# Batch 1's k and q permutes made available 0.7 later in the planner's list for ScalarE, in an attention kernel with a two-layer MLP

## The chip, the cores and the metric

The kernel runs on one core of one Trainium2 chip. The metric is the device time of one execution in microseconds. A lower time is better. The profile is one execution of the same program, taken by the hardware profiler; its span runs from the first to the last profiled instruction.

## The reference

Inputs are q, k and v with 8 batches, 8 heads, 576 rows and head width 64, a norm gain of width 64, a layer-norm gain of width 512 and two weight matrices of 512 x 2048 and 2048 x 512, all in float32. Cut to what matters:

```python
kv  = einsum('bhsd,bhse->bhde', k, v)          # 64 x 64 per batch and head
out = einsum('bhsd,bhde->bhse', q, kv)
out = out / sqrt(mean(out*out, -1) + 1e-6) * g_norm
x   = out.transpose(0, 2, 1, 3).reshape(8, 576, 512)
xn  = (x - mean(x)) / sqrt(var(x) + 1e-6) * g_ln
y   = x + maximum(xn @ w_ch1, 0) @ w_ch2       # 8 x 576 x 512
```

## The kernel before, in words

The 8 x 576 = 4608 rows are cut into 36 tiles of 128 rows. Each batch gives four full tiles, and the last 64 rows of two neighbouring batches share a fifth one (`TILES`, lines 75 to 79). Tiles 0 to 3 belong to batch 0, tiles 4 to 7 to batch 1, tile 8 holds the two fifths, and tile 9 is the first of batch 2. Four tiles make a block. Blocks 0 and 1 are "fine": their first MLP layer runs tile by tile (`m1_fine`, L629, 16 matmuls of 128 columns per group). Later blocks run it for four tiles at once (`m1_block`, L644). The second layer is `m2` (L663, four matmuls of 512 columns per group).

A batch needs these steps ahead of the MLP. Its k, v and q are loaded by DMAs that POOL issues and that convert to bf16. For batches 0 to 2 the loads put several rows of one head side by side, and a copy then permutes them to the order the matmuls need: `k_permute` (L404, into `kp`) and `q_permute` (L410, into `qp`), both through the helper `copy`, so that all of them show as L400 on ScalarE. `kv_mm` (L456, matmuls at L461) multiplies k with v, and `kv_out` (L469) puts the result into `kv_pack`. The q tiles are transposed, on TensorE with a copy out of PSUM (`q_turn_pe`, L420, and `q_turn_out`, L400 or L402) or by a transposing DMA that SP issues (`q_turn_dma`, L442). Then `t_out` (L484) multiplies the turned q with `kv_pack`, and squares (`t_sq`, L510), their sums (L519), a root (L523), the scaling (L546 or L550) and the centring (L572) give `xc`. This is turned to `xT` (L579 and L586 for tiles 0 to 11, a DMA at L590 later), which is the input of the first layer. `t_s2` (L596, tile `junk`) takes squares for the variance.

For batch 1, `plan_batch` makes two `k_permute` steps of four heads each, keyed `p - 18`, and four `q_permute` steps of one tile each, keyed `p - 17`, `p - 14`, `p - 11` and `p - 8`, where p is 32. Tiles 0 and 1 of q are turned on TensorE: VectorE copies the first out of PSUM and ScalarE the second. Tiles 2 and 3 are turned by one DMA, which needs the last two permutes. The buffer `qb` that these permutes read is loaded again for batch 2 once the last of them has read it (`qread`, line 774); batch 2's two q permutes (line 789) wait for that load with a lag of 4.0.

The order on each engine is not written out by hand. Every step is given to `add` with an engine, the time that it holds the engine (`occ`), the time until its result can be used (`dur`), a key and its dependencies, and `run_plan` (L108) plays the program through with these estimates. At each turn it takes, over all engines, the step that could start first. On one engine, among steps that could start at the same moment, the lowest key wins. A step that could start up to 0.35 later (`NEAR`) is preferred where its key is lower by more than 0.7 and the other step would get in its way; on PE this holds only for keys below -3. Between keys 16 and 32 the main matmul groups go strictly in their order. DMAs are modelled as one server that works them off in order of issue (`server`). Where a step depends on a DMA, its `lag` is added to the modelled landing:

```python
r = max(r, d.done + (s.lag if d.dma else 0.0))
```

The steps are then emitted in order of their planned start, so the plan fixes only the order on each engine and each DMA queue. On the chip each instruction runs when its engine has come to it and its data are there. PSUM has four banks for matmul groups (tag `mm`), two for `out` and two for `kvt`, and a step that takes a bank also waits for the step that frees it (`frees`).

Of the kernel before, what the change touches and what calls it, by code (L numbers as in the profile page):

```python
# [14 lines left out]
def kernel(  # L15
# [11 lines left out]
    nc = tc.nc  # L27
# [38 lines left out]
    def no_fifth(b):  # L66
        return fifth(b + 1)
# [30 lines left out]
    def add(eng, occ, dur, key, deps, fn, dma=None, alloc=None, main=False, lag=0.0):  # L98
        s = Step()
        s.eng, s.occ, s.dur, s.key, s.fn = eng, occ, dur, key, fn  # L100
        s.deps = [d for d in deps if d is not None]
        s.dma, s.alloc, s.main, s.frees, s.behind = dma, alloc, main, None, None
        s.start = s.done = None
        s.lag = lag
        steps.append(s)
        return s
# [80 lines left out]
    def act_cost(n):  # L187
        return n / 1400 + 0.115, n / 1400 + 0.23
# [51 lines left out]
    def kv_view(buf, b):  # L240
        if b < 2:
            return buf[b % 2][0:96, :].rearrange("p (h t d) -> p h t d", h=H, t=6)
        return buf[b % 2][:, 0:H * 4 * D].rearrange("p (h t d) -> p h t d", h=H, t=4)
# [43 lines left out]
    lag = [("a", 4), ("a", 5), ("b", 4), ("a", 6), ("b", 5), ("a", 7), ("b", 6), ("b", 7)]  # L287
# [59 lines left out]
    def pool_do(occ, fn, deps=()):  # L347
        return add("POOL", occ, occ + 0.1, 0, deps, fn)
# [49 lines left out]
    def copy(eng, o, i):  # L398
        if eng is nc.scalar:
            eng.copy(o, i)  # L400
        else:
            eng.tensor_copy(o, i)  # L402

    def k_permute(eng, b, h0, h1):  # L404
        src = kv_view(kb, b)
        t = src.shape[2]
        copy(eng, kp[b % 2][0:src.shape[0], 0:t, h0:h1, :],
             src[:, h0:h1, :, :].rearrange("p h t d -> p t h d"))

    def q_permute(eng, b, t0, t1):  # L410
        copy(eng, qp[b % 2][:, t0:t1, :, :],
             qb[:, :, t0:t1, :].rearrange("p h t d -> p t h d"))
# [15 lines left out]
    def add_q_turn_pe(b, t, deps, key, eng, h0=0, h1=H):  # L428
        w = (h1 - h0) / H
        s = add("PE", 0.24 * w, 0.24 * w + 0.26, key, [ident] + list(deps), lag=2.0 if t == 4 else 0.0, fn=  # L430
                lambda: q_turn_pe(b, t, h0, h1), alloc=("mm", "kvt")[b])
        occ, dur = act_cost(512 * w) if eng == "ACT" else dve_cost(512 * w, 1.92)
        e = add(eng, occ, dur, key, [s],
                lambda: q_turn_out(b, t, h0, h1, nc.scalar if eng == "ACT" else nc.vector))
        s.frees = e
        adone[b].setdefault(("qT", t), []).append(e)
        return s
# [10 lines left out]
    def add_q_turn_dma(b, t0, t1, deps, key):  # L448
        s = add_dma("SP", key, deps, lambda: q_turn_dma(b, t0, t1), 520.0 * (t1 - t0), 1.0,
                    occ=0.6 * (t1 - t0) + 0.1, lat=0.25, tail=0.42)  # L450
        for t in range(t0, t1):
            adone[b].setdefault(("qT", t), []).append(s)
        if t0 == 4:
            late_turns.append(s)
# [266 lines left out]
    def plan_batch(b):  # L721
        p = pos[FIRST[b]]
        ok = okey[FIRST[b]]
        kperm = []
        if b == 1:
            for h0, h1 in ((0, 4), (4, 8)):
                kperm.append(add("ACT", 1.2, 1.35, p - 18, load["k", 1],
                                 lambda h0=h0, h1=h1: k_permute(nc.scalar, 1, h0, h1)))
            for t in range(5):
                key = (p - 17 + 3 * t) if t < 4 else pos[8] - 40  # L730
                if t < 4:
                    qperm = add("ACT", *act_cost(512), key, load["q", 1],
                                lambda t=t: q_permute(nc.scalar, 1, t, t + 1))
                    qread = qperm
                else:
                    qperm = load["q", 1, 4][0]
                if t < 2:
                    add_q_turn_pe(1, t, [qperm, z1[1]], key + 1, ("DVE", "ACT")[t % 2])
                elif t > 2:
                    add_q_turn_dma(1, *((2, 4) if t == 3 else (4, 5)), [qperm, z1[1]],  # L740
                                   key + 1 if t == 3 else pos[8] - 29)
            vdeps = load["v", 1]
            adone[1]["qread"] = qread
            adone[1]["qfree"] = adone[1]["qT", 4][0]
        else:
            f = FIRST[b]
            def gate(n):

                if b >= 3:
                    m, i = divmod(n, 4)  # L750
                    pool_do(0.1, lambda: nc.gpsimd.tensor_copy(  # L751
                        mark, blk[m]["xT"][:, 0, i * 128:i * 128 + 1]), done[n]["xT"])
            def gate_turn():
                if b >= 3:
                    pool_do(0.1, lambda: nc.gpsimd.tensor_copy(
                        mark, att[b - 1]["qT"][:, 0, 0:1]), [adone[b - 1]["qfree"]])
            dk = [adone[b - 2]["kvmm"]]
            if b < 4:

                pool_do(0.5, lambda: nc.gpsimd.memset(kp[b % 2][no_fifth(b), 4, :, :], 0.0), dk)  # L760
            gate(f - 8 if b > 3 else 5)
            gate_turn()
            by_slot = b >= 3
            if by_slot:
                pool_load(("k", b), load_slots(kp[b % 2], k, b), rate1, dk)
            else:
                pool_load(("k", b), load_kv(kb, k, b), rate4, dk)
            pool_load(("k", b), load_fifth(kp[b % 2][:, 4, :, :], k, b), 180.0, dk)
            def some_q():
                gate(f - 7 if b > 3 else 6)  # L770
                if by_slot:
                    pool_load(("q", b), load_slots(qp[b % 2], q, b), rate1, [adone[b - 2]["qfree"]])
                else:
                    pool_load(("q", b), load_q(b, 0, 4), rate4, [adone[b - 1]["qread"]])
                pool_load(("q", b), load_fifth(qp[b % 2][:, 4, :, :], q, b), 180.0,
                          [adone[b - 2]["qfree"]])
            def some_v():
                gate(f - 6 if b > 3 else 7)
                pool_load(("v", b), load_kv(vb, v, b), rate4, dk)
                pool_load(("v", b), load_fifth(v5[b % 2], v, b), 100.0, dk)  # L780
            for load_some in (some_v, some_q) if b == 2 else (some_q, some_v):
                load_some()
            for h0, h1 in ((0, 4), (4, 8))[by_slot * 2:]:
                kperm.append(add("ACT", 0.85, 1.0, ok - 16, load["k", b][0:1] + dk,
                                 lambda h0=h0, h1=h1: k_permute(nc.scalar, b, h0, h1)))
            qperm = []
            for t0, t1 in ((0, 2), (2, 4))[by_slot * 2:]:
                qperm.append(add("ACT", 0.85, 1.0, ok - 14, load["q", b][0:1] + [
                    adone[b - 2]["qfree"]], lambda t0=t0, t1=t1: q_permute(nc.scalar, b, t0, t1)))
            for x in kperm + qperm:  # L790
                x.lag = 4.0 if b == 2 else 6.0
            kperm += load["k", b]
            turn = add_dma("SP", ok - 12, qperm + load["q", b] + (
                adone[b - 3].get("outs", []) if b >= 3 else []),
                           lambda: q_turn_dma(b), 2.6e3, 1.0, occ=2.98, lat=0.25, tail=0.42)
            for t in range(5):
                adone[b]["qT", t] = [turn]
            adone[b]["qfree"] = turn
            turn.lag = 5.0 if by_slot else 0.0
            adone[b]["qread"] = qperm[-1] if qperm else None  # L800
            vdeps = load["v", b]
        outs_before = adone[b - 3].get("outs", []) if b >= 3 else []
        s = add("PE", 1.12 if b > 1 else 1.34, 1.35 if b > 1 else 1.57, (p - 17.5 if b == 1 else ok - 4), vdeps + kperm,
                lambda: kv_mm(b, range(HP)), alloc="kvt")
        a = add("DVE", 0.34, 0.38, (p - 17 if b == 1 else ok - 2), [s, z1[4], z1[5]] + outs_before,
                lambda: kv_out(b, 0, HP, nc.vector, False))
        a2 = add("DVE", 0.34, 0.38, (p - 17 if b == 1 else ok - 2), [a], lambda: kv_out(b, 0, HP, nc.vector, True))
        s.frees = a2
        s.lag = 5.0 if b > 2 else 2.0 if b == 2 else 0.0
        adone[b]["kvmm"] = s  # L810
        adone[b]["kv"] = [a2]
# [243 lines left out]
```

## Time and profile before

| what | value |
| --- | --- |
| median of 4 runs | 293.45 us (292.79 to 294.83) |
| the profiled execution's own time | 293.36 us |
| its span | 291.6 us |
| PE busy | 284.2 us (97%) |
| PE weight loads busy | 161.7 us (55%) |
| DVE busy | 165.0 us (57%) |
| ACT busy | 142.5 us (49%) |
| POOL busy | 66.4 us (23%) |
| granted TensorE clock | 0.999 |

The page names engines as PE (TensorE), PEld (its weight loads), DVE (VectorE), ACT (ScalarE), POOL (GpSimd) and SP (SyncE, which here only issues DMAs). A line of a timeline gives the start, the duration, the engine, the source line, the operation, the tile it writes and the tile it reads; an idle time ahead of it stands in brackets with what ended it. The chain of work that ended last is followed back from the last instruction. PE's matmul ends are modelled, so the distance between the starts of two groups says more than the end of one.

### The profile page before, as it was taken

The page shows a single profiled execution, that of the slowest core. Times are in us where ns is not written, and L with a number is a line of the kernel's source. Part 1 is how long each engine was busy: PE and PEld are TensorE (multiplying, and loading weights), DVE is VectorE, ACT ScalarE, POOL GpSimd, SP SyncE. Part 2 cuts the span into 40 slices and gives each one's busy share as a digit, 9 for nine tenths or more (in the row PEclk, how much of TensorE's full clock was granted, in tenths as well). Part 3 has the DMA queues.
Part 4 walks back from the last instruction along what each step waited for, and adds up shares of the span by engine and source line. Part 5 has one row for each costly group of instructions (what it writes and reads, how often), then busy time and mean ns, then how long its engine had stood idle before and what let it go on. Part 6 is the DMA issues. An engine that isn't in the chain of part 4 may idle for free.

```text
span 291.6 us, 5221 instructions
## 1 busy us (share of the span) xinstructions
PE 284.2 (97%) x2074; PEld 161.7 (55%) x2074; DVE 165.0 (57%) x362; ACT 142.5 (49%) x288; POOL 66.4 (23%) x93
## 2 busy tenths in 40 slices
PE   8889999999999999999999999999999999999995
PEld 6779845977645445444544445444544444444444
DVE  2586039487973997557755775477557755320022
ACT  2379954788756512761276126612761177016400
POOL 8974231007309005403160405000000000000000
PEclk9999999999999999999999999999999999999999
DMA  7999999948999989996999299912101310120012
GB/s 97 182 199 205 204 199 180 243 78 98 182 222 92 170 117 193 133 176 152 133 132 190 64 202 112 181 55 92 54 18 56 90 54 18 58 93 13 2 72 73
DMA packets 108716, 35.60 MB, mean 122 GB/s; under 512 B 87187, under 2 KB 104467, under 8 KB 108692
## 3 DMA queue, kind: packets, MB, share of 16 engines
q0 software_dynamic: 72624, 18.35, 67.6%
q1 hardware_dynamic: 35828, 16.79, 25.6%
q8 instruction: 16, 0.26, 0.3%
q10 hardware_dynamic: 240, 0.13, 0.2%
q14 instruction: 8, 0.07, 0.1%
HBM read 36.70 MB, written 9.44 MB: 158 GB/s over the span
## 4 chain that ended last, share of the span: by engine, by line
PE 85%; DMA 7%; POOL 6%; issue 0%; ACT 0%; DVE 0%; POOLq 0%
PE mm_ps L663 41%; PE mm_ps L644 33%; DMA qb<-in_q_dram 7%; PE mm_ps L629 5%; PE out_ps L484 3%; PE kv_ps L461 2%; POOL qp L270 1%; POOL w L354 1%; POOL vb L249 1%; POOL kb L249 1%; PE xT_ps L579 1%; POOL w L356 1%; PE qT_ps L420 0%; ACT qp L400 0%; POOL identity masks.py:197 0%
## 5 line engine op out<-in xcount | busy, mean ns | idle before, releaser
L663 PE MATMUL mm_ps<-w,m 128*128 128x512 bf16 (+2 forms) x608 | 129.6, 368 | 0.0
L644 PE MATMUL mm_ps<-xT,w 128*128 128x512 bf16 x448 | 100.6, 379 | 0.0
L651 ACT ACTIVATE m<-mm_ps 128x512 bf16<-128x512 f32 x112 | 66.8, 598 | 50.8 <-PE mm_ps L644 49.9
L663 PEld LDWEIGHTS <-m 128*128 128x128 bf16 x608 | 57.2, 98 | 60.6
L644 PEld LDWEIGHTS <-w 128*128 128x128 bf16 x448 | 43.1, 98 | 48.9
L519 DVE TENSOR_REDUCE ss<-sq 128x8 f32<-128x512 f32 (+1 forms) x37 | 24.8, 670 | 48.1 <-ACT sq L510 48.0
L670 DVE SCALAR_TENSOR_TENSOR x<-mm_ps,rstd,x 128x512 f32<-128x512 f32 (+2 forms) x38 | 27.3, 719 | 40.6 <-PE mm_ps L663 40.6
L510 ACT ACTIVATE sq<-out_ps 128x512 f32<-128x512 f32 (+1 forms) x37 | 21.6, 584 | 45.5 <-PE out_ps L484 45.5
L629 PE MATMUL mm_ps<-xT,w 128*128 128x128 bf16 x512 | 30.6, 219 | 0.0
L629 PEld LDWEIGHTS <-w 128*128 128x128 bf16 x512 | 29.2, 98 | 0.8
L572 DVE SCALAR_TENSOR_TENSOR xc<-x,mv,gl 128x512 bf16<-128x512 f32 (+1 forms) x38 | 27.3, 723 | 1.2
L514 DVE TENSOR_TENSOR xg<-out_ps,gn 128x512 f32<-128x512 f32 x34 | 23.2, 683 | 0.2
L636 ACT ACTIVATE m<-mm_ps 128x512 bf16<-128x512 f32 x32 | 18.4, 598 | 3.0 <-PE mm_ps L629 2.9
L751 POOL COPY mark<-xT 128x1 bf16<-128x1 bf16 x15 | 6.9, 460 | 56.3 <-DMA xT<-xc 50.8
L523 ACT ACTIVATE rms<-ss,eps_attn 128x8 f32<-128x8 f32 (+1 forms) x37 | 11.1, 300 | 14.5 <-DVE ss L519 14.5
L550 DVE TENSOR_TENSOR x<-xg,inv 128x512 f32<-128x512 f32 x24 | 16.6, 692 | 0.8
L566 DVE BATCH_NORM_STATS2 stats<-x 128x6 f32<-128x512 f32 x24 | 16.6, 690 | 0.5
L484 PEld LDWEIGHTS <-qT 128*128 128x128 bf16 x160 | 11.4, 98 | 6.8 <-ACT qT L400 0.8
L484 PE MATMUL out_ps<-kv_pack,qT 128*128 128x128 bf16 x160 | 14.5, 219 | 0.4 <-ACT qT L400 0.3
L472 DVE CAST kv_pack<-kv_ps 64x256 bf16<-64x256 f32 x14 | 5.9, 422 | 11.9 <-PE kv_ps L461 11.8
L461 PEld LDWEIGHTS <-kp 128*128 128x128 bf16 (+1 forms) x168 | 10.1, 98 | 2.5 <-issue 0.4
L277 POOL DMA_DIRECT2D qp<-in_q_dram x5 | 11.2, 2235 | 0.8 <-issue 0.8
(69 smaller groups left out, 181.6 us busy)
## 6 DMA issues: line engine op xcount, KB each, us to landing
out_dram<-x SPq DMA_DIRECT2D x30, 256.0 KB, 2.6
w<-in_moe_w_ch_dram POOLq DMA_DIRECT2D x8, 512.0 KB, 12.4
vb<-in_v_dram POOLq DMA_DIRECT2D x6, 512.0 KB, 10.9
kp<-in_k_dram POOLq DMA_DIRECT2D x5, 512.0 KB, 8.6
qp<-in_q_dram POOLq DMA_DIRECT2D x5, 512.0 KB, 10.1
out_dram<-x SPq DMA_DIRECT2D x10, 128.0 KB, 2.3
qb<-in_q_dram POOLq DMA_DIRECT2D x2, 512.0 KB, 18.5
qp<-in_q_dram POOLq DMA_DIRECT2D x10, 64.0 KB, 9.2
```

The source lines that it names most:

```text
L484: nc.tensor.matmul(o3[:, hp, :], lhsT=att[b]["qT"][:, 4 * t + hp, :], rhs=kv_pack[b % 3][:, hp, :], start=(i == 0), stop=(i == len(bs) - 1))
L510: nc.scalar.activation(sq[:, h0:h1, :], st[n]["ps", h0][:, h0:h1, :], func=AF.Square)
L514: nc.vector.tensor_mul(xg[:, h0:h1, :], st[n]["ps", h0][:, h0:h1, :], gn.to_broadcast([128, h1 - h0, D]))
L519: nc.vector.tensor_reduce(ss[:, h0:h1, :], st[n]["sq"][:, h0:h1, :], axis=AX.X, op=ALU.add)
L550: nc.vector.tensor_mul(x, xg, inv)
L572: nc.vector.scalar_tensor_tensor(xc[:, f0:f1], in0=st[n]["x"][:, f0:f1], scalar=blk[m]["mv"][:, i, 0:1], in1=gl[:, f0:f1], op0=ALU.subtrac ...
L629: nc.tensor.matmul(ps[:, d, :], lhsT=w1[c][:, kk, d * 128:(d + 1) * 128], rhs=blk[m]["xT"][:, kk, i * 128:(i + 1) * 128], start=(kk == 0), ...
L636: nc.scalar.activation(st[n]["m1"][:, c, :, :], st[n]["m1ps", c], func=AF.Relu)
L644: nc.tensor.matmul(ps, lhsT=w1[c][:, kk, d * 128:(d + 1) * 128], rhs=blk[m]["xT"][:, kk, :], start=(kk == 0), stop=(kk == nKm - 1))
L651: nc.scalar.activation(blk[m]["m1", c][:, d, :], blk[m]["m1ps", g], func=AF.Relu)
L663: nc.tensor.matmul(st[n]["m2ps", f0], lhsT=m1_piece(n, c, d), rhs=w2[c][:, d, f0:f1], start=(c == 0 and d == 0), stop=(c == 3 and d == 3))
L670: nc.vector.scalar_tensor_tensor(x[:, f0:f1], in0=st[n]["m2ps", f0], scalar=blk[m]["rstd"][:, i, :], in1=x[:, f0:f1], op0=ALU.mult, op1=AL ...
```

## The change

The two k permutes and the four q permutes of batch 1 get `lag=0.7`, where they had none. The planner then takes their data to be there 0.7 after the modelled landing of the load. No instruction is added or removed, and no cost estimate or key is altered. Everything that differs on the chip is an order of instructions on the engines and queues, as far as the planner comes to another one.

```diff
         if b == 1:
             for h0, h1 in ((0, 4), (4, 8)):
                 kperm.append(add("ACT", 1.2, 1.35, p - 18, load["k", 1],
-                                 lambda h0=h0, h1=h1: k_permute(nc.scalar, 1, h0, h1)))
+                                 lambda h0=h0, h1=h1: k_permute(nc.scalar, 1, h0, h1), lag=0.7))
             for t in range(5):
                 key = (p - 17 + 3 * t) if t < 4 else pos[8] - 40
                 if t < 4:
                     qperm = add("ACT", *act_cost(512), key, load["q", 1],
-                                lambda t=t: q_permute(nc.scalar, 1, t, t + 1))
+                                lambda t=t: q_permute(nc.scalar, 1, t, t + 1), lag=0.7)
                     qread = qperm
```

## The prediction

> **What bounds the kernel now.** I read the page first: span, busy shares and the chain's shares.
>
> ```profile
> span 291.6 us, 5221 instructions
> ...
> PE 284.2 (97%) x2074; PEld 161.7 (55%) x2074; DVE 165.0 (57%) x362; ACT 142.5 (49%) x288; POOL 66.4 (23%) x93
> ...
> PE 85%; DMA 7%; POOL 6%; issue 0%; ACT 0%; DVE 0%; POOLq 0%
> ```
>
> PE is the bound. Next, the chain in order of time, around the place the change touches.
>
> ```profile
> 18.97 0.24 issue
> 19.21 19.70 DMA qb<-in_q_dram
> 38.91 0.02 issue
> 38.93 0.63 ACT qp L400
> 39.56 0.05 issue
> 39.61 0.40 PE qT_ps L420 x4
> 40.00 0.86 PE mm_ps L663 x4
> 40.87 0.22 PE out_ps L484 x4
> ```
>
> From 39.61 to 288.06 every piece of the chain is PE, one after the other. So a microsecond of new PE idleness after 39.61 costs a microsecond, and nothing there can be won by order. The only thing to win is the step before it: PE waits for the first q permute of batch 1, which waits for a load. Third, the timelines of PE and ACT.
>
> ```profile
> 33.28 1.03 PE L663 MATMUL mm_ps<-w,m 128*128 128x512 bf16 x4
> 34.14 1.50 PE L461 MATMUL kv_ps<-vb,kp 96*128 96x128 bf16 x24
> 35.49 3.62 PE L663 MATMUL mm_ps<-w,m 128*128 128x512 bf16 x16
> 39.61 0.40 PE L420 MATMUL qT_ps<-identity,qp 128*128 128x128 bf16 x4 [0.50 <-ACT qp L400]
> ```
>
> ```profile
> 29.50 1.09 ACT L636 ACTIVATE m<-mm_ps 128x512 bf16<-128x512 f32 x2
> 30.90 1.47 ACT L400 COPY kp<-kb 96x1536 bf16<-96x1536 bf16 x1 [0.31 <-DMA kb<-in_k_dram]
> 32.28 1.07 ACT L636 ACTIVATE m<-mm_ps 128x512 bf16<-128x512 f32 x2
> 33.24 1.46 ACT L400 COPY kp<-kb 96x1536 bf16<-96x1536 bf16 x1
> 38.93 2.17 ACT L400 COPY qp<-qb 128x512 bf16<-128x512 bf16 x4 [1.55 <-DMA qb<-in_q_dram]
> 41.35 0.59 ACT L400 COPY qT<-qT_ps 128x512 bf16<-128x512 bf16 x1 [0.24 <-PE qT_ps L420]
> 60.05 1.99 ACT L400 COPY qp<-qb 128x1024 bf16<-128x1024 bf16 x2
> ```
>
> PE's idle time: a group of four L663 matmuls takes 0.864 (the chain's 1.73 for eight), so sixteen from 35.49 are issued by 38.95; the next instruction starts at 39.61. That is 0.66 us, of which the bracket counts 0.50 after the modelled end. The ACT rows show both loads landing with ACT already idle: 0.31 for k, 1.55 for q.
>
> **The new order, worked by hand.** The change acts through the planner, so I carried its rules through by hand from the costs in the code. Its dates (called "planned") serve to find the order only; durations below are the profile's. In the old plan k lands at 30.19 and q at 38.27, while the trace has 30.9 and 38.91: the plan is 0.65 to 0.7 early, and the lag moves it there.
>
> *k permutes.* The first becomes possible at planned 30.95 instead of 30.25. The eviction of tile 3's first MLP group is possible at 31.06 with key 13 against 14, inside the 0.35 window, so it goes first. On ACT the order becomes eviction, permute, eviction, permute, two evictions. From the rows: PE gives tile 3's first group at 28.81 + 2 x 0.893 + 0.2 (latency to ACT, as at L636's waits) = 30.8; eviction pitch 0.48; permute pitch 1.38 (30.90 to 32.28). The permutes start at 31.28 and 33.14, and the second ends at 34.60 (34.70 before). The eviction fills ACT's 0.31 idle; the sum on ACT is 0.1 us shorter, and no PE wait depended on it.
>
> *kv product.* Its planned readiness moves from 34.26 to 34.63, past the end of the first `m2` group at 34.32, so the second `m2` group goes ahead of it. On the chip: `m2` 34.14, kv at 35.00 to 36.35, with its inputs there since 34.60. Its copies to `kv_pack` (two, 0.86 together) end near 37.6; `t_out` of tile 4 needs them after 41. Cost nothing, cover 3 us.
>
> *q permutes.* Planned 39.03 instead of 38.33. PE has a free turn at 39.12 with nothing but the next `m2` group to run; the first q turn goes behind it. PE before: m2, turn 0, m2, out 4, turn 1, m2, m2, out 5. After: m2, m2, turn 0, turn 1, m2, out 4, out 5, m2. On the chip the moved group runs 38.94 to 39.80, over the whole wait. Turn 0 has its data (39.56). Turn 1 comes at 40.02 and needs the second permute: starts are (2.17 - 0.61)/3 = 0.52 apart, so it ends at 38.93 + 0.52 + 0.61 = 40.06, and with 0.05 to PE it is a wait of 0.09. Out 4 at 41.20 needs VectorE's copy of turn 0 (39.80 + 0.43 + 0.42 = 40.65), out 5 at 41.42 ScalarE's copy of turn 1 (40.11 + 0.42 + 0.59 = 41.12). Both are there.
>
> So PE gains 0.66 - 0.09 = 0.57 us. Bounds: 0 if another wait follows at once, and 0.86 (the whole moved group) in an execution where q lands later than 38.91.
>
> *What moves with them: the last q permute, SP and POOL.* ScalarE's copy of turn 1 (key 19 against 24) goes ahead of the fourth permute, which then runs 41.01 to 41.62 instead of ending at 41.10. Two queues wait for it: SP's transposing DMA of q tiles 2 and 3, and POOL's load of batch 2's q into the same buffer.
>
> ```profile
> 41.13 1.33 SPq L442 DMA_TRANSPOSE qT<-qp  x1
> ```
>
> ```profile
> 42.03 0.89 POOL L256 DMA_DIRECT2D qb<-in_q_dram  x1 [1.59 <-ACT qT L400]
> ```
>
> The transpose is issued 0.5 later. Issue to landing of these was 5.0 to 8.8 us in this trace, so it is there by 50.5; `t_out` 6 runs after 53. No cost. The load was issued 0.93 after the permute ended and may now be issued between 41.65 and 42.55; it took 17.3 us to land (59.33), and its readers started at 60.05.
>
> In the planner the swap counts for more. Old planned starts: SP's transpose 40.42, the load 40.79 (held by its DMA lane). New: both at the same instant, and the tie goes to POOL, which is looked at first. The modelled server then puts the 2.66 us load ahead of the transpose. Planned landing of q tiles 2 and 3 goes from 52.56 to 55.22, and batch 2's q gets there 1.04 sooner. Two orders follow. `t_out` 6 and 7 go behind two more groups on PE (53.36 before; 55.46 after, in chip time less the 0.57). ScalarE's squares of tile 6 move from 55.39 to about 55.9, `xc` of tile 6 ends near 59.8, and its turn has its place at 60.70 - 0.57 = 60.13: covered by 0.3. And batch 2's two q permutes are placed on ScalarE before `junk` of tile 5 and the squares of tile 7, about 1 us earlier. On the chip they will then wait for the load: issued at 42.0, landed at 59.3, permutes until 61.25 (1.89 for two), `junk` 0.63, copy of `xT` 6 0.59, so 62.5. Tile 6's first group wants it at 63.51 - 0.57 = 62.94. Covered by 0.45.
>
> One more tight place: VectorE takes y of tiles 1 and 2 ahead of `xc` of tile 5; y of tile 3, which frees a bank, ends near 51.75 against 51.89 for the group that takes the bank. Between 0 and 0.2 us; I take 0.
>
> A rule of the Trainium skill bears on the swap. The rows are the landing times above: the short transposes land in 5.0 to 8.8 us while the loads beside them take 17.3 or more, so a transpose does not stand behind a whole load. DMA: Bandwidth & Descriptors, section Queues, rings and completion order, says that each DMA engine goes round-robin over queue rows, a packet at a time. By the rows the swap costs nothing, as taken; by the planner's single server it would put q tiles 2 and 3 up to 2.66 us later, still ahead of 53, so the sum stays.
>
> A second rule speaks against the change: TensorE: Matmul & The Clock Gate, section Architectural detail, calls ScalarE's queue strictly first-in, first-out. What stands behind batch 2's permutes then cannot pass while they wait for their load; the trace shows such a stop at 38.93 (1.55 idle). By the rule with no cover, the wait from 58.4 to 59.3 would come off the gain, 293.8; with the cover of 0.45 worked out above it stays 292.9.
>
> **The sum.** The profiled execution took 293.36 us, 1.76 outside its span of 291.6. 293.36 - 0.57 = 292.79; the median of the runs lies 0.09 above that execution: about 292.9 us. A difference under 0.5% (1.47 us) is about what a measurement here can't tell from no change, so this is "same".
>
> **The rivals.**
>
> *Nothing moves or the wait only changes place.* If PE's 0.66 us goes to another wait right behind (turn 1, the bank of y 3, `xT` 5), the time is 293.2 to 293.5. For it: covers of 0.1 to 0.45 are thin. Against: three rows would have to be late together. 12%.
>
> *Slower: batch 2's q permutes stop ScalarE.* Place: ScalarE from about 58.4 (60.05 less 1.04 and 0.57); behind them `xT` 6. The stall on PE is (landing - 59.80), one to one. It decides against the change at a landing of 59.80 + 0.57 = 60.37, and makes over 0.5% at 61.84. The other load into this buffer took 19.70 instead of 17.3: issued at 42.03 that is 61.73, a stall of 1.93, and 293.36 + 0.09 - 0.57 + 1.93 = 294.8; issued at 42.55 it is 295.3. For it: the planner believes in 54.66 plus a lag of 4.0 where the chip had 59.33. Against: 17.3 is this load's own row, and the page shows the DMA engines running dry just then, so that the landing is set by what is queued and not by a few tenths of issue time. The slice with the 4 begins at 58.3 us (40 slices of 7.29):
>
> ```profile
> DMA  7999999948999989996999299912101310120012
> ```
>
> With the many orders after 60 that also change and that I can't all follow (each wait there is paid in full), 15% for over 0.5%.
>
> *Faster by over 0.5%.* It needs 1.47 us, and PE has 0.66 of idleness left to remove, 0.86 with a late q. Only a run-to-run difference gets there: 5%.
>
> **Numbers.** The forecast's case, 68%, own range 292.4 to 293.2. Same 68 + 12 = 80%, slower 15%, faster 5%. The 8-in-10 range goes from 292.2 (gain 0.86 and the spread of runs, lowest 0.66 under their median) to 294.8 (the stall by the longer load).
>
> **What would show it.** Right: the PE timeline has two `m2` groups before the kv product, four after it, then both q turns together and no bracket at the first; the chain no longer passes through the q load; `t_out` 6 and 7 stand near 55.5. Wrong: a bracket at L629 near 63 that names `xT`, a bracket at L484 near 67 that names SP's transpose, or the first q turn still waiting for ScalarE. The prediction fails if the planner, by a tie that I resolved wrongly, orders blocks 1 and 2 so that PE meets a new wait of over 2 us.

## The result, and the profile after

The changed kernel takes 293.9 us (median, 292.96 to 297.02) against 293.17 us for the kernel before, measured beside it. The ratio is 1.0023, with a 95% interval of 1.0014 to 1.0032: a loss of 0.7 us, inside the 0.5% that was called "same", but a loss where a gain of 0.6 was forecast. The profiled execution took 293.65 us, 1.75 outside its span. The profiled executions of two kernels below, e12 and g1, ran at a granted clock of 0.758 and 0.564, so no profile of these two is used.

The page of the changed kernel, span, busy shares and the chain's shares:

```profile
span 291.9 us, 5221 instructions
...
PE 285.6 (98%) x2074; PEld 162.5 (56%) x2074; DVE 164.2 (56%) x362; ACT 142.5 (49%) x288; POOL 66.0 (23%) x93
...
PE 85%; DMA 8%; ACT 2%; DVE 2%; POOL 1%; issue 1%; DVEq 0%; POOLq 0%
```

PE's busy share has gone up with the same 2074 matmuls, so it cannot show this loss. The chain can: ScalarE has 2% of it where it had none. Its lines from 40 us on, in order of time (start, duration, what):

```profile
40.33 0.58 ACT qT L400
40.91 0.53 ACT qp L400
41.44 0.30 issue
41.74 18.00 DMA qb<-in_q_dram
59.74 0.02 issue
...
60.72 1.04 ACT qp L400
61.76 0.98 ACT m L636 x2
62.74 0.49 ACT sq L510
63.22 0.48 ACT xT L586
63.71 0.04 issue
63.75 3.73 PE mm_ps L629 x64
```

Before, everything from 39.61 to 288.06 was PE. Now the chain leaves PE at the first q turns and comes back at 63.75, by way of the fourth q permute of batch 1, the load of batch 2's q into the same buffer, that batch's two permutes, and what stands behind them on ScalarE. The timeline of PE (start, duration, engine, line, operation, tiles, count, idle time ahead in brackets):

```profile
33.16 1.89 PE L663 MATMUL mm_ps<-w,m 128*128 128x512 bf16 x8
34.88 1.50 PE L461 MATMUL kv_ps<-vb,kp 96*128 96x128 bf16 x24
36.23 3.62 PE L663 MATMUL mm_ps<-w,m 128*128 128x512 bf16 x16
39.68 0.61 PE L420 MATMUL qT_ps<-identity,qp 128*128 128x128 bf16 x8
...
53.45 0.39 PE L461 MATMUL kv_ps<-vb,kp 128*128 128x128 bf16 x4
53.86 0.22 PE L461 MATMUL kv_ps<-v,kp 128*128 128x128 bf16 x1
...
59.63 0.92 PE L484 MATMUL out_ps<-kv_pack,qT 128*128 128x128 bf16 x8
60.39 1.03 PE L663 MATMUL mm_ps<-w,m 128*128 128x512 bf16 x4
...
61.47 1.89 PE L663 MATMUL mm_ps<-w,m 128*128 128x512 bf16 x8
63.75 3.73 PE L629 MATMUL mm_ps<-xT,w 128*128 128x128 bf16 x64 [0.39 <-ACT xT L586]
...
83.40 0.81 PE L644 MATMUL mm_ps<-xT,w 128*128 128x512 bf16 x3
```

The first four lines are the predicted order, and the first q turn has no bracket any more. Then PE stands still in four new places, by the starts: 0.19 in batch 2's kv product (53.45 + 0.22 to 53.86, for the last v rows), 0.31 at the out of tile 8 (eight matmuls take 0.45, here 59.63 to 60.39), 0.55 ahead of tile 6's first group (61.47 + 1.73 = 63.20 to 63.75), and 0.12 at the outs of tiles 9 and 10. ScalarE around it:

```profile
57.67 0.29 ACT L523 ACTIVATE rms<-ss,eps_attn 128x8 f32<-128x8 f32 x1
59.76 1.99 ACT L400 COPY qp<-qb 128x1024 bf16<-128x1024 bf16 x2 [1.80 <-DMA qb<-in_q_dram]
61.66 1.07 ACT L636 ACTIVATE m<-mm_ps 128x512 bf16<-128x512 f32 x2
62.63 0.60 ACT L510 ACTIVATE sq<-out_ps 128x512 f32<-128x512 f32 x1
63.10 0.60 ACT L586 COPY xT<-xT_ps 128x512 bf16<-128x512 bf16 x1
```

It idles for 1.80 us at the head of the permutes, and two evictions of tile 5 (copies of matmul results out of PSUM), a square and the copy of `xT` 6 stand behind them. In the kernel before, all evictions of tile 5 stood ahead of the permutes, and the copy directly behind them. Two rows of ScalarE there, and PE's first group of tile 6:

```profile
58.47 0.60 ACT L636 ACTIVATE m<-mm_ps 128x512 bf16<-128x512 f32 x1 [0.29 <-PE mm_ps L629]
...
61.94 0.59 ACT L586 COPY xT<-xT_ps 128x512 bf16<-128x512 bf16 x1
```

```profile
63.51 3.74 PE L629 MATMUL mm_ps<-xT,w 128*128 128x128 bf16 x64
```

**The yardstick.** Between the first `m2` group (L663) and the first group of block 2 (L644) PE does the same work in every kernel of this study. Where it never waits there, it needs 49.07 us; that is the least of all profiles, and four reach it exactly. What is above is waiting. Behind block 2's start nothing differs: 291.6 - 83.03 before, 291.9 - 83.40 after, 291.0 - 82.54 in an experiment, 208.5 each time. So the stretch accounts for all of the change: 83.03 - 33.28 = 49.75 before, 0.68 of waiting, all of it at the first q turn; 83.40 - 33.16 = 50.24 after, 1.17 of waiting, none of it there. In these two profiles 0.68 was won and 1.17 paid for it.

### The profile page after: what moved, and what is told of

It is laid out like the page before. It is cut to its first block, busy times and chain, and to the rows that moved or that the text cites. A ratio compares the mean times of both kernels' runs of the same rounds, so it can differ in the third digit from the quotient of the medians.

```text
span 291.9 us, 5221 instructions
## 1 busy us (share of the span) xinstructions
PE 285.6 (98%) x2074; PEld 162.5 (56%) x2074; DVE 164.2 (56%) x362; ACT 142.5 (49%) x288; POOL 66.0 (23%) x93
## 4 chain that ended last, share of the span: by engine, by line
PE 85%; DMA 8%; ACT 2%; DVE 2%; POOL 1%; issue 1%; DVEq 0%; POOLq 0%
PE mm_ps L663 38%; PE mm_ps L644 33%; PE mm_ps L629 7%; DMA qb<-in_q_dram 6%; PE kv_ps L461 3%; PE out_ps L484 2%; DMA vb<-in_v_dram 2%; PE xT_ps L579 1%; DVE xc L572 1%; ACT qp L400 1%; POOL kb L249 1%; POOL vb L249 0%; DVE x L546 0%; ACT qT L400 0%; ACT m L636 0%
## 5 line engine op out<-in xcount | busy, mean ns | idle before, releaser
L663 PE MATMUL mm_ps<-w,m 128*128 128x512 bf16 (+2 forms) x608 | 129.8, 368 | 0.0
L644 PE MATMUL mm_ps<-xT,w 128*128 128x512 bf16 x448 | 100.6, 379 | 0.0
L663 PEld LDWEIGHTS <-m 128*128 128x128 bf16 x608 | 57.1, 98 | 60.4
L644 PEld LDWEIGHTS <-w 128*128 128x128 bf16 x448 | 43.1, 98 | 48.8
L629 PE MATMUL mm_ps<-xT,w 128*128 128x128 bf16 x512 | 30.6, 219 | 0.4 <-ACT xT L586 0.4
L629 PEld LDWEIGHTS <-w 128*128 128x128 bf16 x512 | 29.2, 98 | 1.4 <-issue 0.7
L751 POOL COPY mark<-xT 128x1 bf16<-128x1 bf16 x15 | 6.4, 425 | 59.5 <-DMA xT<-xc 53.1
L484 PE MATMUL out_ps<-kv_pack,qT 128*128 128x128 bf16 x160 | 14.5, 219 | 0.2
L461 PEld LDWEIGHTS <-kp 128*128 128x128 bf16 (+1 forms) x168 | 10.7, 101 | 2.4 <-DMA vb<-in_v_dram 0.5
L461 PE MATMUL kv_ps<-vb,kp 128*128 128x128 bf16 (+1 forms) x144 | 11.4, 227 | 0.6 <-DMA vb<-in_v_dram 0.6
```

The source lines that it names most:

```text
L461: nc.tensor.matmul(ps[:, hp, :], lhsT=kp[b % 2][p, t, 2 * hp:2 * hp + 2, :].rearrange("p h d -> p (h d)"), rhs=(v5[b % 2][:, 2 * hp:2 * hp ...
L484: nc.tensor.matmul(o3[:, hp, :], lhsT=att[b]["qT"][:, 4 * t + hp, :], rhs=kv_pack[b % 3][:, hp, :], start=(i == 0), stop=(i == len(bs) - 1))
L629: nc.tensor.matmul(ps[:, d, :], lhsT=w1[c][:, kk, d * 128:(d + 1) * 128], rhs=blk[m]["xT"][:, kk, i * 128:(i + 1) * 128], start=(kk == 0), ...
L644: nc.tensor.matmul(ps, lhsT=w1[c][:, kk, d * 128:(d + 1) * 128], rhs=blk[m]["xT"][:, kk, :], start=(kk == 0), stop=(kk == nKm - 1))
L663: nc.tensor.matmul(st[n]["m2ps", f0], lhsT=m1_piece(n, c, d), rhs=w2[c][:, d, f0:f1], start=(c == 0 and d == 0), stop=(c == 3 and d == 3))
```

## Where the order went another way

Worked through with the kernel's own planner (its dates again for order only), four things come out:

- The k permutes keep their old order on ScalarE. `junk` of tile 3, key 17, was free at planned 30.683, so the 0.35 window closed 0.024 before the eviction at 31.057 became possible. Only the kv product of batch 1 moves. This costs nothing.
- On PE the `m2` groups and q turns come in the predicted order, and the tie between SP's transpose and POOL's load at planned 41.917 goes to POOL, as predicted. `t_out` 6 and 7 move back as predicted.
- Not predicted: I let tile 5's first group take PE at planned 53.82, but that group waits for a PSUM bank until 54.207. Batch 2's kv product is possible at 54.064 and slips in, five groups earlier than before. It now comes just when the last v rows land.
- Hence tile 5's evictions come 1.1 later in the plan, and batch 2's q permutes go ahead of two of them.

The out of tile 8 has the same work of PE ahead of it as before. PE comes to it at 59.63 instead of 60.25, and its turned q, which SP issued at 51.87, landed 8.1 us later, at 59.97. In the profile of before it was issued at 52.24 and took 7.6: it was there at 59.84, with PE 0.41 behind it.

So the change has two parts: the gain at the first q turns, and, through the tie, a new order from 53 us on, called the new tail below. The experiments take them apart.

## The experiments

The table has, for each kernel, where PE reaches block 2 and its waiting in the stretch (one profiled execution each), when batch 2's q landed (POOL's issue plus the time to landing), and the times. The ratio is an estimate over all runs and not the quotient of the two medians; in e4 the medians alone give 1.0014.

| kernel | block 2 | waiting | q landed | median, before beside it | ratio, 95% interval |
| --- | --- | --- | --- | --- | --- |
| before | 83.03 | 0.68 | 59.33 | 293.17 | |
| changed | 83.40 | 1.17 | 59.74 | 293.9, 293.17 | 1.0023 (1.0014 to 1.0032) |
| changed, e4 | 83.69 | 1.24 | 59.99 | 293.79, 293.39 | 1.0000 (0.9983 to 1.0018) |
| changed, e12 | | | | 294.06, 293.14 | 1.0013 (0.9995 to 1.0031) |
| changed, f1 | 83.11 | 0.81 | 59.41 | 293.86, 293.44 | 1.0019 (0.9999 to 1.0039) |
| changed, f2 | 83.62 | 0.99 | 59.94 | 293.65, 293.44 | 1.0008 (0.9995 to 1.0021) |
| gain, old tail, e1 | 82.54 | 0.00 | 59.35 | 292.93, 293.39 | 0.9983 (0.9969 to 0.9998) |
| gain, old tail, e11 | 82.23 | 0.00 | 58.77 | 292.85, 293.14 | 0.9986 (0.9971 to 1.0000) |
| new tail alone, e10 | 82.90 | 0.64 | 59.23 | 293.26, 293.14 | 1.0004 (0.9988 to 1.0020) |
| new tail alone, f1 | 82.87 | 0.17 | 58.99 | 293.81, 293.44 | 1.0017 (1.0004 to 1.0031) |
| new tail alone, f2 | 82.97 | 0.44 | 59.28 | 293.38, 293.44 | 1.0000 (0.9981 to 1.0020) |

Profiles of some executions begin the stretch later, since PE was held by loads earlier on (in e8, below, 1.21 us at 16.92); a late start hides the first q turn's wait, so block 2's date is read beside the waiting. That wait also differs between executions that start alike: in the kernels that keep the old first q turn it was 0.66 before, 0.68 with k only, and 0.16 to 0.35 in e9, e10, f1, f2 (new tail alone) and g2. So the 0.66 of the first profile is at the upper end of what can be won there.

### One part of the lag alone, and the change again

```diff
 # q only (e2), from the kernel before: lag=0.7 on the four q permutes alone
-    lambda t=t: q_permute(nc.scalar, 1, t, t + 1))
+    lambda t=t: q_permute(nc.scalar, 1, t, t + 1), lag=0.7)
 # k only (e3), from the changed kernel: the same line the other way
```

> The lag of 0.7 on the four q permutes alone, none on the k permutes. Theory A: all of the effect is in the q permutes, so as the changed kernel, 293.7 to 294.1 us, ratio 1.002. A rival, that the later place of batch 1's kv product on PE costs: 293.2 or below.

> The lag of 0.7 on the two k permutes alone, none on the q permutes. ScalarE's order is that of the kernel before; on PE only the kv product of batch 1 goes behind one m2 group. Theory A: the 0.66 us wait of PE at the first q turn stays, nothing else moves, 293.1 to 293.3 us, ratio 1.000. The rival, that the moved kv product costs: 293.6 or more.

> The changed kernel once more, beside the others on the same chip. Theory A: 293.9 us, ratio 1.002, and a profile in which PE waits at the same places (kv product of batch 2, out of tile 8, first group of tile 6), with lengths that move from execution to execution as the loads land earlier or later, 0.5 to 2 us in sum. If the waits of the first profile were an accident of one execution, they would be absent or elsewhere.

q only: 293.98 (1.0014, 0.9993 to 1.0034). k only: 293.13 (0.9987, 0.9973 to 1.0002). In k only, ScalarE's order is that of before, and the wait that was to go is still there; two lines of its PE timeline:

```profile
36.26 2.75 PE L663 MATMUL mm_ps<-w,m 128*128 128x512 bf16 x12
39.53 0.40 PE L420 MATMUL qT_ps<-identity,qp 128*128 128x128 bf16 x4 [0.52 <-ACT qp L400]
```

The times alone do not settle it, since both intervals hold 1. The orders do: q only has both q turns together (at 40.95) and batch 2's kv product early (54.72), k only has neither (kv product at 59.05). So what the change does it does through the lag of the q permutes. The change made once more (e4: 293.79, 1.0000) shows that its waits trade places. In e4 the last v rows landed 1.2 later and PE paid at the kv product; that time the copy of `xT` 6 was there in time:

```profile
53.70 0.39 PE L461 MATMUL kv_ps<-vb,kp 128*128 128x128 bf16 x4
55.14 0.22 PE L461 MATMUL kv_ps<-v,kp 128*128 128x128 bf16 x1 [1.06 <-DMA v<-in_v_dram]
...
64.17 3.74 PE L629 MATMUL mm_ps<-xT,w 128*128 128x128 bf16 x64
```

### The gain with the old tail

```diff
-        free = dict.fromkeys(("PE", "ACT", "DVE", "POOL", "SP"), 0.0)
+        free = dict.fromkeys(("PE", "ACT", "DVE", "SP", "POOL"), 0.0)
```

The changed kernel, with SP looked at ahead of POOL where both could start at the same moment. The tie goes the other way, and the order behind it stays the old one.

> The changed kernel, with one thing altered in the planner: where two engines could start at the same planned moment, SP is looked at ahead of POOL, so that the modelled DMA server works off the transpose of batch 1's q tiles 2 and 3 before the load of batch 2's q, as it did before the change. The lags stay. Theory A (the loss comes from the tie: it reorders what follows planned 53, and PE then waits for batch 2's fifth v, for the turned q of tile 8 and for xT of tile 6): the order after planned 53 is that of the kernel before, these waits are gone, PE keeps the 0.57 to 0.66 us won at the first q turn, and the time is 292.5 to 292.7 us, ratio about 0.998. Theory B (whatever the order, PE comes 0.66 us earlier to data that are not there yet): the waits stay, 293.2 or more, ratio 1.000 or above. Theory C (the moved kv product and q turns of batch 1 cost by themselves): about 293.9, as changed.

> The changed kernel with the tie decided for SP once more, to narrow the interval. Theory A: ratio 0.997 to 0.999, 292.6 to 292.9 us, no wait of PE between the first q turn and the first group of block 2.

Both are faster than the kernel before: 0.9983 (0.9969 to 0.9998) and 0.9986 (0.9971 to 1.0000, which just touches 1), 0.3 to 0.5 us. Both intervals lie below the changed kernel's 1.0014 to 1.0032. PE's timeline of e1, the first q turns, kv product, tile 6's first group and block 2:

```profile
39.99 0.61 PE L420 MATMUL qT_ps<-identity,qp 128*128 128x128 bf16 x8
...
58.65 0.39 PE L461 MATMUL kv_ps<-vb,kp 128*128 128x128 bf16 x4
...
63.02 3.74 PE L629 MATMUL mm_ps<-xT,w 128*128 128x128 bf16 x64
...
82.54 1.67 PE L644 MATMUL mm_ps<-xT,w 128*128 128x512 bf16 x7
```

And ScalarE of e1 at batch 2's permutes:

```profile
59.57 1.99 ACT L400 COPY qp<-qb 128x1024 bf16<-128x1024 bf16 x2
61.45 0.59 ACT L586 COPY xT<-xT_ps 128x512 bf16<-128x512 bf16 x1
```

No bracket anywhere. The permutes stand behind all evictions of tile 5 and directly ahead of the copy, so a load that landed at 59.35 holds nobody. The forecast's 292.9 is this kernel's time: it is what the gain is worth when nothing takes it back, though from 293.39 and 293.14 beside it and not from 293.45. It is also the fastest version of the study, by the turn of one tie.

### The new tail without the gain

```diff
-            return r + 0.06
+            return r + (0.6 if s.eng == "SP" and s.key == 25 else 0.06)
```

The kernel before, with SP's transpose of q tiles 2 and 3 planned late enough that POOL's load goes first. No permute is lagged; from planned 53 on the order is the changed kernel's.

> The kernel before, no lag, with one thing altered in the planner: SP's transpose of batch 1's q tiles 2 and 3 may start 0.54 later in the plan, so that the modelled server works off the load of batch 2's q first. From planned 53 on the order is then that of the changed kernel; the first q turn stays where it was. Theory A (the order after 53 costs, and PE's end there is set by the landing of batch 2's loads): about as late as the changed kernel although it lacks the 0.66 us gain, or a little later, 293.7 to 294.4 us, ratio 1.001 to 1.004, with waits at the same places. Theory B (only the earlier PE creates the waits): 293.2 to 293.4, ratio 1.000, no wait.

> The swap alone once more (order of the changed kernel from planned 53, no lag). Theory A (the loads' landing sets the end in both): as late as the changed kernel beside it, 293.7 to 294.1 us; the first run of it (293.26) was lucky, and its profiles now show the wait at the early kv product. Theory D (the later fourth permute, and with it the later transpose and load behind it, also delay the landing of batch 2's v and q in the changed kernel, so that both parts are needed for the loss): 293.2 to 293.5 again, with the last rows of batch 2's v there when PE comes to them.

> A further sample of the swap alone, as above: theory A 293.7 to 294.1 us, theory D 293.2 to 293.5 us.

1.0004, 1.0017 (1.0004 to 1.0031) and 1.0000: at most a small loss, clear of 1 in one of three. By the middle values that is less than the new tail takes from the changed kernel, which falls from 0.998 to between 1.0000 and 1.0023 by it; the intervals overlap. Theory A's times were missed twice and met once (293.81). In its profiles ScalarE does idle for the load (0.62 to 1.20 us) with the same work behind it, but PE mostly finds its data there: behind the first q turn it waits 0.39, 0.01 and 0.24, against 0.8 to 1.2 in the changed kernel. Two things differ. PE came to batch 2's kv product at 53.73 to 54.10, against 53.45 to 53.85 in the changed kernel, some 0.3 later. And the loads had landed earlier: the last v rows at 52.89 to 53.73 against 53.83 to 55.07, q as in the table. How much each of the two saves is not separated. ScalarE of f2:

```profile
59.33 1.99 ACT L400 COPY qp<-qb 128x1024 bf16<-128x1024 bf16 x2 [0.97 <-DMA qb<-in_q_dram]
61.23 1.08 ACT L636 ACTIVATE m<-mm_ps 128x512 bf16<-128x512 f32 x2
62.20 0.60 ACT L510 ACTIVATE sq<-out_ps 128x512 f32<-128x512 f32 x1
62.67 0.60 ACT L586 COPY xT<-xT_ps 128x512 bf16<-128x512 bf16 x1
```

The copy ends at 63.27, PE wanted it at 61.56 + 1.73 = 63.29.

The repeats of the changed kernel beside these runs:

> The changed kernel a third time, on the same chip as the kernel with the swap alone and the one with the tie decided for SP. Theory A: ratio 1.001 to 1.003, 0.8 to 1.2 us above the one with the tie decided for SP, the waits again between 53 and 70.

> The changed kernel beside it. Both theories: 293.7 to 294.1 us. Theory A: batch 2's last v rows and q land no later than in the swap alone. Theory D: they land 0.3 to 1.2 us later.

> A further sample of the changed kernel, as above: 293.7 to 294.1 us by both theories.

Their ratios are 1.0013, 1.0019 and 1.0008; none is a gain, and none of the repeats, e4 with them, is clear of 1 by itself. The loss of 0.2% rests on the first and longest measurement (54 runs).

### Each half of the new tail, in and out

```diff
 # e5, changed kernel, batch 2's q permutes back: lag 5.04 for 4.0
-                x.lag = 4.0 if b == 2 else 6.0
+                x.lag = (5.04 if x in qperm else 4.0) if b == 2 else 6.0
 # e6, changed kernel, batch 2's kv product back
-        s.lag = 5.0 if b > 2 else 2.0 if b == 2 else 0.0
+        s.lag = 5.0 if b > 2 else 2.5 if b == 2 else 0.0
 # e7, changed kernel with both of these
 # e8, kernel before, q permutes forward: 2.96 in the place of 5.04
 # e9, kernel before, kv product forward: key 35.5 for batch 2
```

> The changed kernel with the lag of batch 2's two q permutes at 5.04 instead of 4.0, which puts them back to their planned place of before (59.76), behind one more eviction of tile 5 and the squares of tile 7. Batch 2's kv product keeps its new early place on PE. Theory A1 (the larger part of the loss is PE standing at the early kv product for the load of batch 2's last v rows and at out of tile 8 for its turned q; these waits were 0.2 to 1.2 and 0.3 us): little is won, 293.5 to 293.9 us, ratio 1.000 to 1.002, and no wait of tile 6's first group. Theory A2 (the larger part is ScalarE's stop at batch 2's q permutes, which makes tile 6's first group wait, 0.55 us in the first profile): 293.0 to 293.3, ratio 0.999 to 1.000.

> The changed kernel with the lag of batch 2's kv product at 2.5 instead of 2.0, so that the product comes again behind the first m2 group of tile 4 (planned 59.09), and out of tile 8 behind it. Batch 2's q permutes stay earlier than in the kernel before (planned 58.98 against 59.76), now behind all evictions of tile 5; out of tiles 6 and 7 stay late. Theory A1: the waits of PE at the kv product, at out of tile 8 and at tile 6 are all gone, the gain at the first q turn stays, 292.6 to 292.9 us, ratio 0.998. Theory A2: ScalarE still stops at the q permutes, tile 6 still waits, 293.2 to 293.5, ratio 1.000.

> The changed kernel with the lag of batch 2's kv product at 2.5 and that of batch 2's q permutes at 5.04: both go back to their planned places of before (59.09 and 59.76); out of tiles 6 and 7 stay three groups late, the last thing that the tie moved. Theory A: the waits at the kv product and at tile 6 are gone; small ones at out of tile 8 and at the turns of tiles 7 and 8 may stay (0.25 and 0.3 us with only the kv product put back), 292.7 to 293.2, ratio 0.998 to 0.9995. If it is not below the kernel before, the late out of tiles 6 and 7 costs by itself.

> The kernel before, with the lag of batch 2's two q permutes at 2.96 instead of 4.0: they come 1.04 earlier in the plan, ahead of junk of tile 5 and the squares of tile 7, as the prediction thought the change would place them; nothing else of the change. From the trace of before: landing at 59.3 to 59.8, permutes 1.89, junk 0.63, copy of xT 0.59, so xT of tile 6 at 62.5 to 62.9, against 63.5 where tile 6's first group takes it. Theory A1: no new wait on PE, 293.2 to 293.4, ratio 1.000. Theory A2: a wait at tile 6's first group, 293.6 or more, ratio 1.001 or above.

> The kernel before, with batch 2's kv product given the key 35.5 instead of 40, so that it runs five groups earlier on PE, ahead of tile 5's first group; nothing else of the change. PE comes to it near 54.7 (53.80 plus 0.89), 1.2 later than in the changed kernel; the load of batch 2's last v rows was there at 53.9 in one profile of the changed kernel and at 55.1 in the other. Theory A1: a wait of 0 to 0.3 us, longer in some executions, 293.3 to 293.7, ratio 1.000 to 1.001. Theory A2: nothing at all, 293.2.

| kernel | waiting, where | ratio, 95% interval |
| --- | --- | --- |
| e5 | 1.33: 0.89 in the kv product, 0.44 around the first q turns, none at tile 6 | 1.0012 (0.9990 to 1.0034) |
| e6 | 0.76: 0.25 at tile 8's out, 0.21 within tile 6's groups, 0.29 at two turns | 1.0000 (0.9982 to 1.0019) |
| e7 | 0.00, with a start at 34.62 | 0.9996 (0.9979 to 1.0012) |
| e8 | 0.00, with a start at 35.11 | 1.0004 (0.9983 to 1.0025) |
| e9 | 0.24 | 0.9998 (0.9977 to 1.0019) |

Either half, left in the changed kernel, brings waits at another place, PE's row of e5 for one:

```profile
54.93 0.22 PE L461 MATMUL kv_ps<-v,kp 128*128 128x128 bf16 x1 [0.72 <-DMA v<-in_v_dram]
```

With both out there is none. But e7's profile starts the stretch 1.4 us late, so its PE comes late to every load, and its time (293.29, just above the 292.7 to 293.2 expected) does not show the gain come back: the interval holds 0.998 and 1 alike. By its time e6 (293.50) missed theory A1's 292.6 to 292.9. Either half put into the kernel before costs nothing that can be measured; e8's profile does not try it, since its load had landed at 57.02, 3 us before the permutes. All five intervals hold 1: times could not tell these kernels apart, and how the loss divides between the halves stays open.

### When batch 2's q lands

In the table q landed at 59.41 to 59.99 in the changed kernel, at 58.99 to 59.28 with the new tail alone. The load was not issued later (41.74 to 42.14 against 41.93 to 42.29) but took longer, 17.5 to 18.0 against 16.7 to 17.3. In the changed kernel the fourth q permute comes behind the copy of turn 1, and with it SP's transpose comes closer to the load. Two kernels move that permute alone:

```diff
 # g1: lag 2.4; g2: lag 3.2
-    lambda t=t: q_permute(nc.scalar, 1, t, t + 1))
+    lambda t=t: q_permute(nc.scalar, 1, t, t + 1), lag=3.2 if t == 3 else 0.0)
```

> The kernel before with a lag of 2.4 on the fourth q permute of batch 1 alone. ScalarE, SP and POOL then have the changed kernel's order throughout and PE has it from 53 us on, but the first q turn keeps its old place and its wait of 0.6. What is asked is why the load of batch 2's q landed 17.5 to 18.0 us after its issue in six profiles of the changed kernel and its near relations, and 16.7 to 17.4 in the kernel before and the swap alone, though it was not issued later (41.74 to 42.14 against 41.93 to 42.29). Theory D: SP's transpose, which here as there goes out close to the load instead of 1.1 to 1.4 us ahead of it, makes it slow; then 17.5 to 18.0 here too, ScalarE's wait for it ends at 59.9 to 60.8, PE reaches block 2 at 83.3 to 84.0, and the time is 293.7 to 294.2. Theory A: the landing scatters and the order of the two does nothing to it; then 16.7 to 17.3, ScalarE's wait ends at 59.0 to 60.0, PE reaches block 2 near 82.9, and the time is 293.2 to 293.6 as with the swap alone.

> The kernel before with a lag of 3.2 on the fourth q permute of batch 1 alone. Every engine and queue then has the order of the swap alone, except that this permute runs on ScalarE behind the copy of turn 1 and one square, so that it ends near 42.7 and SP's transpose goes out near 42.8 (40.6 to 41.0 with the swap alone). Theory D: the load of batch 2's q lands 17.5 us or more after its issue, and as it may be issued up to 0.8 later too, ScalarE's wait ends at 60.3 to 61.0; PE reaches block 2 at 83.5 to 84.3 and the time is 293.9 to 294.5. Theory A: it lands 16.7 to 17.3 us after its issue; ScalarE's wait ends at 59.2 to 60.2, later than with the swap alone only by what the issue is later; PE reaches block 2 at 82.9 to 83.3 and the time is 293.2 to 293.8.

g1: 293.72 us, 1.0016 (1.0000 to 1.0033). g2: 293.88 us, 1.0021 (1.0007 to 1.0036), though PE's order is that of the new tail alone. POOL's row of the load in g2:

```profile
42.82 0.89 POOL L256 DMA_DIRECT2D qb<-in_q_dram  x1 [2.81 <-ACT qp L400]
```

The view of its landing (KB, then us from issue to landing), ScalarE and PE of g2:

```profile
qb<-in_q_dram POOLq DMA_DIRECT2D x1, 512.0 KB, 17.0
```

```profile
59.81 1.99 ACT L400 COPY qp<-qb 128x1024 bf16<-128x1024 bf16 x2 [1.66 <-DMA qb<-in_q_dram]
```

```profile
63.80 3.73 PE L629 MATMUL mm_ps<-xT,w 128*128 128x128 bf16 x64 [0.43 <-ACT xT L586]
```

The load took 17.0, with SP's transpose 0.28 ahead of it, as close as in the changed kernel (41.46 and 41.74). So a transpose close ahead need not make it slow; in this theory D of these expectations missed. But the late permute held the issue itself until 42.82, the load landed at 59.82, and PE waited 0.59 for tile 6 and was at block 2 at 83.45, as late as the changed kernel. One wait of PE follows the landing one to one here. Tile 6's first group starts 4.0 us after it wherever that wait is the last to end (two permutes 1.90, two evictions and a square 1.44, the copy 0.60, and 0.07 of starts): 63.75 - 59.74 = 4.01 in the changed kernel, 4.04 in its profile f2, 4.03 in e10, 3.98 in g2. Block 2 starts 19.65 later, and 208.5 + 1.75 later the execution ends: 59.74 + 4.01 + 19.65 + 208.5 + 1.75 = 293.65, the profiled time.

**What is shown and what is open.** Shown: the gain at the q turns (gone wait, and a faster kernel where the tail is old); that the new tail takes it back, with waits that end when a DMA lands; that the same tail alone costs less, by the middle values. Open: why the load took 17.5 to 18.0 us in the four profiles of the changed kernel. Scatter is not excluded: e1, e5, e6, e7 and e11 have the same order up to planned 53 and took 16.8 to 17.7. All nine with that order lie between 16.8 and 18.0 (the middle one 17.6), the nine with another between 15.3 and 17.4 (the middle one 17.0): the ranges overlap, and 0.6 between the middles may be the order or chance.

## Why the prediction was wrong, step by step

- *PE is the bound, and only the wait at the first q turn can be won:* right, 0.68 of waiting in the stretch, all there.
- *q permutes:* right in kind, a little too large. Both turns come together behind the sixth `m2` group, the wait of 0.66 is gone, and so is the 0.09 that turn 1 was to wait. The gain by itself measured 0.3 to 0.5 us (e1, e11) against 0.57; the wait that goes was 0.16 to 0.68 long in different executions, and the prediction had one profile of it.
- *k permutes:* the order on ScalarE was wrong, for want of `junk` 3 among the candidates. The window of 0.35 counts from the earliest candidate. It carried no term of the sum.
- *The tie, and `t_out` 6 and 7:* right. That the late outs cost nothing by themselves fits e7, where they stay late and PE waits nowhere; but that profile starts late, so it is not settled. The rows behind it were read loosely: of the loads beside the transposes the last v rows took 14.1 us, not 17.3 or more.
- *"Two orders follow":* here it failed. A third followed, batch 2's kv product five groups earlier. Its price was 0.19 to 1.22 us in the profiles of the changed kernel, and it moved two evictions of tile 5 behind batch 2's permutes. The step passed over a bank that tile 5's first group waits for, 0.39 in the plan, with another matmul ready to take its place. The out of tile 8 (0.31) was not priced at all: PE came 0.62 earlier to a turned q that landed 0.13 later, and 0.41 was the cover.
- *"Covered by 0.45":* mis-sized. Landing 59.74 in the place of 59.3 (0.44), and two evictions and a square (61.66 to 63.10, 1.44) in the place of `junk` (0.63): the copy ended at 63.70, not 62.5. Tile 6's group wanted it at 63.20, not at 62.94, since PE had waited before. 0.45 - 1.2 + 0.26 is -0.5; the trace has -0.55, with the bracket at L629 near 63 that names `xT`, one of the prediction's own signs of being wrong.
- *The rival "slower"* had this mechanism at this place, but put the deciding landing at 60.37. With 4.0 us from landing to tile 6, not 3.2, a landing of 59.5 already puts tile 6's group at its old place (63.51 - 4.0) and uses up the gain; the load's own row is 59.33, and the changed kernel had 59.41 to 59.99.
- *The second skill rule:* TensorE: Matmul & The Clock Gate, section Architectural detail, has ScalarE strictly first-in, first-out. The trace agrees: the evictions at 61.66 had their matmuls done by 58.8 and stood behind a load. The 293.8 that the rule gave without cover came close by luck: it counted 0.9, where ScalarE idled 1.80 and PE lost 0.55 to it beside other waits.
- *The range* held 293.9, by the wide bound of the load.

## What to carry to other kernels

On an engine that is 97% busy, a wait that goes makes everything behind it earlier, and every load that was just in time becomes late by that much: before counting the gain, list the loads that land within it and what stands behind their readers. Where a planner sets the order, a small lag can flip a tie far away; follow the candidates for each free turn, banks included, and not only the step that was delayed. If an unrelated tie turns, try it the other way: here that was the difference between a loss of up to 0.2% and a gain of 0.15%. And a wait for a load is not one number: look at it in several executions before it becomes a gain.

## What was not expected of the hardware

- Four profiles of one kernel have the same load landing 17.5 to 18.0 us after its issue, and its neighbour, the last v rows, 14.5 to 15.3. PE then waits once at the one, once at the other. One profile would have named one culprit.
- DMA: Bandwidth & Descriptors, section Queues, rings and completion order, describes round-robin over queue rows. The short transpose landed in 8.9 us in the changed kernel (8.8 before), at 50.36, ahead of the last v rows, which POOL had issued at 39.33 and which landed at 53.83; so it did not stand behind a whole load, as the rule has it. SP's row of its issue:

```profile
41.46 1.33 SPq L442 DMA_TRANSPOSE qT<-qp  x1
```

That is still ahead of the load of batch 2's q at 41.74. The swap in the plan never took place on the chip, and no run here shows a transpose issued behind that load; all of the swap's cost came from the order that the planner made of it.
